# First transform stage: the kernel row of each pair ahead of its signal row, from row 4 on

## The chip, the cores and the metric

The kernel runs on one core of a Trainium2 chip. The time is device microseconds of one execution of the whole program. A core has five engines that work side by side: TensorE (matmuls; PE in the profile, its weight loads PEld), VectorE (DVE), ScalarE (ACT), GpSimd (POOL) and SyncE (SP). Each takes its own instructions in the order in which they were built. SP, ScalarE and GpSimd also issue DMA transfers.

## The reference

Four residual layers, A, B, A, B, on `x` of 2048 rows and 576 columns, each on the layer-normed `x`:

```python
def _A_ref(x, ...):                      # Fourier mixing
    a = einsum("bsd,ed->bse", x, dft_hid_re)
    b = einsum("bsd,ed->bse", x, dft_hid_im)
    return einsum("ts,bse->bte", dft_seq_re, a) - einsum("ts,bse->bte", dft_seq_im, b)

def _B_ref(q, k, v, shift_k, ssm_k, ssm_D):
    k_shift = short causal convolution of k with 4 taps
    kv = k_shift * v
    y = causal convolution of kv with ssm_k over all 2048 rows, by FFT
    return q * (y + kv * ssm_D)          # q is the layer-normed x
```

The long convolution depends on `k`, `v` and `ssm_k` alone and not on `x`. So the kernel computes it once, as a side branch, while the first A layer runs.

## The kernel before

Every float32 operand of a matmul is taken as a high part and a low part. `split` (lines 97 to 99) makes them: ScalarE rounds the source to the high part, and then VectorE subtracts it from the source to get the low part. The products high by high, high by low and low by high are accumulated.

**The main line.** `layer` runs steps n = 0, 1, 2, ...; a step multiplies one 128-row slice of `x` by one 128 by 512 tile of the sequence matrix. `load_c` (L168 is its DMA on SP) fetches the tile into a raw buffer and splits it. It is called two steps ahead and has three split buffers. The text writes C(n) for the tile of step n. A step has 14 matmuls (tiles `s` and `rm` in the profile). Blocks of 16 steps end with the evacuation of the sums into `u`.

**The side branch.** `branch` is a generator. Until step 42 the main loop takes pieces from it after half steps and whole steps, by a fixed schedule (`F1_16`, `F1_END`). Its first stage, the one that is changed, handles 16 rows j of two kinds: the signal row (src 0, `v` times the short convolution of `k`) and the kernel row (src 1, `ssm_k`). The list `todo` gives their order, one entry for two pieces. Rows 0 to 3 (`K_FIRST` = 4) come kind by kind, one row at a time. From row 4 on the two kinds of a row follow each other, and are multiplied together as a pair.

- `f1_loads` (L418 is the load of a row, on SP) keeps three entries ahead. There are three landing buffers (`land`), used in turn, so the load of an entry waits until the third entry before it has been read for the last time. With a row's first entry comes its matrix, by GpSimd (L172).
- `f1_split` makes the parts. For a signal row VectorE first multiplies the landed `v` into the convolved row, in place (L426); this is the last reader of its landing buffer. For a kernel row the last reader is the subtraction of the split. A pair of rows shares one buffer (`xp`, two of them); the first entry of a pair takes it.
- `f1_products` multiplies: a group of six matmuls into two of three PSUM banks (`bf`), two evacuations by ScalarE (L451) and one store to `td` on ScalarE's queue (L452). A pair has three groups of 384 columns, and their turn is set in `visits`, from three half steps behind the pair's second entry on. A row of the first four has two groups of 288 columns.
- `convolve` is the short convolution on VectorE: multiplies at L393, adds at L398. Its operations are spread evenly until the next signal row needs them; `later` in the main loop of the stage finds that row in `todo`. L374 loads `k`.

The order in which each engine gets its instructions is not the order of the source alone: the framework moves an instruction that it expects to be ready ahead of another one. The built order of each engine is fixed before the run.

Of the kernel before, what the change touches and what calls it, by code (L numbers as in the profile page):

```python
# [19 lines left out]
J = S // P  # L20
# [10 lines left out]
K_FIRST = 4  # L31
# [34 lines left out]
def fnet_h3_kernel(ctx: ExitStack, tc: tile.TileContext, x, c_mat, w_re, w_im, k_pad, v, shift_k,  # L66
# [30 lines left out]
    def split(h, l, src):  # L97
        a = nc.scalar.activation(h, src, AF.Copy).ins  # L98
        return a, nc.vector.tensor_tensor(l, src, h.bitcast(F32), OP.subtract).ins  # L99
# [43 lines left out]
    def two(v):  # L143
        return v.rearrange("p (a n) -> p a n", a=2)
# [197 lines left out]
    def parts(i):  # L342
        v = ring[i]()
        return v[:, :D], v[:, D:]
# [4 lines left out]
    def branch():  # L349
# [49 lines left out]
                        yield  # L399

        todo = [(1, 1), (0, 1)] + [(j, 1) for j in range(2, K_FIRST)] + [(j, 0) for j in range(K_FIRST)]
        todo += [(j, src) for j in range(K_FIRST, J) for src in range(2)]
        loads = [0]

        def f1_loads(upto):
            while loads[0] < min(upto, len(todo)):
                j, src = todo[loads[0]]
                loads[0] += 1
                if j not in fcs:
                    fcs[j] = two(ring["fc"]())  # L410
                    if pows:
                        load_fr(fcs[j], f1c[j])
                    else:
                        raw = two(tmp[:, :2 * P])
                        nc.sync.dma_start(raw, f1c[j])
                        nc.scalar.activation(fcs[j], raw, AF.Copy)
                landed[j, src] = ring["land"]()
                nc.sync.dma_start(landed[j, src], (ssm_k if src else v)[:, j, :])  # L418
                if src and j == 0:
                    nc.sync.dma_start(tmp[:1, D:], ssm_d[None, :])  # L420

        def f1_split(j, src):
            r = landed.pop((j, src))
            if not src:
                row = rows[j // 2][:, j % 2, :]
                nc.vector.tensor_tensor(row, row, r, OP.mult)  # L426
                r = row
            elif j == 0:
                nc.vector.tensor_tensor(r[:1], r[:1], tmp[:1, D:], OP.add)
            if j < K_FIRST:  # L430
                xf = parts("xf")
                parted[:] = split(xf[0], xf[1], r)
                return xf
            if not src:
                t = ring["xp"]()
                paired[:] = t[:, :2 * D], t[:, 2 * D:]
            h, l = (t.rearrange("p (a s d) -> p a s d", a=2, s=2)[:, :, src, :] for t in paired)
            parted[:] = split(h, l, two(r))
            return tuple(paired)
# [15 lines left out]
        def visit(half):  # L455
            if visits and visits[0][0] <= half:
                f1_products(*visits.pop(0)[1:])

        for n, (j, src) in enumerate(todo):
            f1_loads(n + 1)  # L460
            if n < 2:
                yield
            xf = f1_split(j, src)
            if j < K_FIRST:
                visits += [(2 * n + 2, j, fcs[j], xf, hf * HD, HD, "so", hf * D + src * HD) for hf in range(2)]
            elif src:
                visits += [(2 * n + 3, j, fcs[j], xf, at, VW, "sp", at) for at in range(0, 2 * D, VW)]
            if n:
                f1_loads(n + 3)
            later = [m for m in range(n + 1, len(todo)) if todo[m][1] == 0 and 7 * (todo[m][0] // 2 + 1) > made_ops]  # L470
            for half in range(2):
                visit(2 * n + half)
                if later and n > 2:
                    left = 7 * (todo[later[0]][0] // 2 + 1) - made_ops
                    for _ in range(-(-left // (2 * (later[0] - n) - half)) if left > 0 else 0):
                        next(conv)
                        made_ops += 1
                yield
# [267 lines left out]
    pending = []  # L746
    lay(flts, SC_AT, ("craw", NT, CRAW))
    br = branch()
    wl = load_w()
    load_x(0)  # L750
# [404 lines left out]
```

## Time and profile before

| | |
|---|---|
| median of 3 runs | 1191.76 us (1188.8 to 1192.48) |
| the profiled execution | 1191.32 us |
| its span | 1189.5 us |
| granted TensorE clock, mean | 0.998 |
| TensorE matmuls busy | 1168.5 us |
| VectorE busy | 872.8 us |
| ScalarE busy | 650.0 us |
| the stage that is changed, from the first pair's first group to its last group | 94.2 to 198.6 us |

A row of the order of time begins with the start in us, then the duration in us, the engine, the line, the operation, the tiles (written <- read), shapes and a count of equal instructions in a row. In brackets stands the idle time of the engine just before, and what ended it. A "q" behind an engine's name marks its queue, which issues a DMA. In the view by windows each engine has its busy us and instructions in the stretch, in the order PE, PEld, DVE, ACT, POOL; the last three figures are the granted clock, the share of the DMA engines and GB/s. In the DMA views the last figure is the median us from issue to landing.

### The profile page before, as it was taken

What the parts mean: (1) busy time and instruction counts of PE and PEld (TensorE: products, weight loads), DVE (VectorE), ACT (ScalarE), POOL (GpSimd) and SP (SyncE); (2) the same over time, 40 slices, a digit from 0 to 9 for tenths busy, and PEclk for the clock granted to TensorE, in tenths of its full rate; (3) what the DMA queues carried; (4) which work ended last, traced back from release to release, by engine and by line L of the source; (5) the groups of instructions that cost most, each with busy time, mean ns of one, the idle gap of its engine ahead of it and who ended that gap; (6) DMA issues with size and microseconds to landing.
All of it is one profiled execution on the core that took longest, in us unless ns stands there. A gap on an engine that the chain in (4) does not pass through costs nothing.

```text
span 1189.5 us, 18071 instructions
## 1 busy us (share of the span) xinstructions
PE 1168.5 (98%) x6184; PEld 987.2 (83%) x6184; DVE 872.8 (73%) x1562; ACT 650.0 (55%) x1279; POOL 75.1 (6%) x116
## 2 busy tenths in 40 slices
PE   7999999999999999999999999999999999999997
PEld 5776767888888888888888898888888888889997
DVE  7899983688777778787767665865776776775764
ACT  7865555567766668766645666534444445450200
POOL 2210000000000000001101111000000000001111
PEclk9999999999999999999999999999999999999999
DMA  9869898545656656648966777772772776795621
GB/s 340 295 197 306 269 290 267 178 139 177 225 189 198 200 160 204 186 137 239 273 197 226 235 246 231 251 250 73 255 248 71 240 273 248 266 322 158 214 83 41
DMA packets 147454, 255.65 MB, mean 215 GB/s; under 512 B 16161, under 2 KB 56353, under 8 KB 147362
## 3 DMA queue, kind: packets, MB, share of 16 engines
q1 hardware_dynamic: 111890, 210.17, 54.9%
q10 hardware_dynamic: 28560, 37.91, 9.1%
q0 software_dynamic: 6912, 6.43, 2.4%
q8 instruction: 48, 0.79, 0.3%
q14 instruction: 44, 0.36, 0.1%
HBM read 187.80 MB, written 66.65 MB: 214 GB/s over the span
## 4 chain that ended last, share of the span: by engine, by line
PE 76%; ACT 2%; DVE 2%; DMA 2%; issue 1%; POOLq 0%; ACTq 0%; DVEq 0%
PE s L75 42%; PE bk L75 29%; PE rm L75 4%; ACT flts L512 1%; ACT mid L512 1%; DMA t<-ud 1%; DVE mid L518 0%; DMA yb<-flts 0%; DMA flts<-vd 0%; DMA flts<-in_c_mat 0%; DVE flts L532 0%; DVE flts L530 0%; ACT u L98 0%; DVE flts L531 0%; DVE flts L533 0%
## 5 line engine op out<-in xcount | busy, mean ns | idle before, releaser
L75 PE MATMUL s<-mats 128*128 128x512 f32 x2088 | 543.0, 395 | 1.6 <-ACT mats L195 0.8
L75 PEld LDWEIGHTS s<-mats 128*128 128x128 f32 x2088 | 381.0, 188 | 83.2 <-issue 10.6
L99 DVE TENSOR_TENSOR mats<-flts,mats 128x512 fp32r<-128x512 f32 x206 | 141.0, 688 | 50.8 <-ACT mats L98 48.4
L98 ACT ACTIVATE mats<-flts 128x512 fp32r<-128x512 f32 x206 | 128.3, 628 | 82.6 <-PE bk L75 31.2
L75 PE MATMUL bk<-mid 128*128 128x288 f32 x704 | 127.7, 302 | 1.6 <-DVE flts L287 0.8
L75 PEld LDWEIGHTS bk<-mid 128*128 128x128 f32 x704 | 108.0, 188 | 23.7 <-ACT flts L512 5.8
L512 ACT ACTIVATE flts<-bk 128x288 f32<-128x288 f32 (+1 forms) x192 | 76.3, 406 | 90.8 <-PE bk L75 75.9
L75 PE MATMUL bk<-w,u 128*128 128x288 f32 x864 | 121.3, 296 | 1.0 <-DVE w L241 0.4
L75 PEld LDWEIGHTS bk<-w,u 128*128 128x128 f32 x864 | 117.3, 188 | 5.5 <-DVE flts L532 1.7
L518 DVE TENSOR_TENSOR mid<-flts,mid 128x576 fp32r<-128x576 f32 (+1 forms) x149 | 93.4, 629 | 18.6 <-ACT mid L512 15.2
L75 PE MATMUL rm<-mats 128*128 128x512 f32 x304 | 94.6, 391 | 0.2 <-ACT flts L512 0.2
L512 ACT ACTIVATE mid<-flts 128x576 fp32r<-128x576 f32 (+1 forms) x148 | 80.3, 575 | 11.8 <-DVE flts L533 8.5
L287 DVE TENSOR_TENSOR flts<-flts,bk 128x288 f32<-128x288 f32 x48 | 21.8, 453 | 65.8 <-PE bk L75 65.7
L451 ACT ACTIVATE flts<-bf 128x384 f32<-128x384 f32 (+1 forms) x104 | 43.2, 463 | 46.0 <-PE bf L75 45.9
L75 PE MATMUL bk<-mats 128*128 128x288 f32 (+1 forms) x376 | 67.8, 317 | 0.0
L75 PEld LDWEIGHTS rm<-mats 128*128 128x128 f32 x304 | 56.9, 188 | 12.8 <-ACT flts L512 0.6
L75 PE MATMUL s<-t,mats 128*128 128x512 f32 x264 | 65.4, 390 | 0.6 <-DVE t L99 0.3
L184 POOL TENSOR_TENSOR flts<-flts 128x1 f32<-128x1 f32 x35 | 28.7, 821 | 522.4 <-DVE flts L183 522.3
L75 PE MATMUL bk<-mats,t 128*128 128x288 f32 (+1 forms) x368 | 59.3, 303 | 0.0
L512 ACT ACTIVATE flts<-flts 64x288 f32<-64x288 f32 x128 | 56.6, 443 | 4.7
L75 PEld LDWEIGHTS s<-t,mats 128*128 128x128 f32 x264 | 49.4, 188 | 11.7 <-DVE t L99 0.8
L75 PEld LDWEIGHTS bk<-mats 128*128 128x128 f32 x376 | 55.5, 188 | 3.4
(146 smaller groups left out, 1496.7 us busy)
## 6 DMA issues: line engine op xcount, KB each, us to landing
flts<-in_c_mat SPq DMA_DIRECT2D x148, 256.0 KB, 3.3
ph<-in_c_mat SPq DMA_DIRECT2D x54, 512.0 KB, 4.5
flts<-in_c_mat SPq DMA_DIRECT2D x30, 512.0 KB, 4.8
flts<-td SPq DMA_DIRECT2D x53, 288.0 KB, 2.9
td<-flts ACTq DMA_DIRECT2D x36, 384.0 KB, 4.6
vd<-flts ACTq DMA_DIRECT2D x64, 144.0 KB, 2.7
flts<-vd SPq DMA_DIRECT2D x32, 288.0 KB, 4.1
ud<-ph ACTq DMA_DIRECT2D x12, 512.0 KB, 6.3
```

The source lines that it names most:

```text
L75: return nc.tensor.matmul(ps, lhsT, rhs, start=first, stop=last, skip_group_check=more).ins
L98: a = nc.scalar.activation(h, src, AF.Copy).ins
L99: return a, nc.vector.tensor_tensor(l, src, h.bitcast(F32), OP.subtract).ins
L184: pows.append(nc.gpsimd.tensor_tensor(rs, ve, mhalf, OP.pow).ins)
L287: added[:] = [nc.vector.tensor_tensor(r[:, cs], r[:, cs], ps[:, :HD], OP.add).ins]
L451: stored[:] = [nc.scalar.activation(so[:, i, :], ps[i], AF.Copy).ins]
L512: last_act.append(nc.scalar.activation(*args, **kw).ins)
L518: nc.vector.tensor_tensor(l, src, h.bitcast(F32), OP.subtract)
```

## The change

From row 4 on, the entry of the kernel row stands ahead of that of the signal row. The kernel row takes the pair's buffer, and the three groups are due behind the signal row.

```diff
         todo = [(1, 1), (0, 1)] + [(j, 1) for j in range(2, K_FIRST)] + [(j, 0) for j in range(K_FIRST)]
-        todo += [(j, src) for j in range(K_FIRST, J) for src in range(2)]
+        todo += [(j, src) for j in range(K_FIRST, J) for src in (1, 0)]
...
-            if not src:
+            if src:
                 t = ring["xp"]()
                 paired[:] = t[:, :2 * D], t[:, 2 * D:]
...
             if j < K_FIRST:
                 visits += [...]
-            elif src:
+            elif not src:
                 visits += [(2 * n + 3, j, fcs[j], xf, at, VW, "sp", at) for at in range(0, 2 * D, VW)]
```

## The prediction

> **What bounds the kernel now.** I read the page first, then the busy time by windows, then the order of time around rows 3 to 6 of the first transform stage, and last the DMA views. Names: a "step" n is the 14 matmuls on one sequence-matrix tile C(n); a "group" is the six matmuls of one call of `f1_products`, numbered 0 to 51 in issue order, so groups 14 and 15 are the two halves of signal row 3, groups 16 to 18 row 4, 19 to 21 row 5. kernel(j) and signal(j) are the two splits of row j; product(j) is the multiply at L426 before signal(j).
>
> ```profile
> span 1189.5 us, 18071 instructions
> PE 1168.5 (98%) x6184; PEld 987.2 (83%) x6184; DVE 872.8 (73%) x1562; ACT 650.0 (55%) x1279; POOL 75.1 (6%) x116
> PE 76%; ACT 2%; DVE 2%; DMA 2%; issue 1%; POOLq 0%; ACTq 0%; DVEq 0%
> ```
>
> ```profile
> 80.00:100.00 20.00, 18.54 (x96) 13.20 (x94) 19.44 (x24) 9.31 (x21) 1.05 (x2) 1.00 0.85 257
> 100.00:120.00 20.00, 20.00 (x102) 14.08 (x99) 20.00 (x23) 11.47 (x24) 1.58 (x3) 1.00 0.98 332
> 180.00:200.00 20.00, 20.00 (x102) 14.08 (x103) 6.86 (x10) 11.78 (x24) 0.53 (x1) 1.00 0.75 242
> ```
>
> TensorE bounds the run; in the stage of the change VectorE (third figure) is nearly as full, and after 180 us it is two thirds idle. How full TensorE really is comes from the starts of the groups:
>
> ```profile
> 79.07 0.68 PE L75 MATMUL bf<-f1r 64*128 64x288 f32 x6
> 80.88 0.66 PE L75 MATMUL bf<-f1r 64*128 64x288 f32 x6 [0.24 <-ACT flts L451]
> 85.79 0.67 PE L75 MATMUL bf<-f1r 64*128 64x288 f32 x6
> 87.29 0.66 PE L75 MATMUL bf<-f1r 64*128 64x288 f32 x6
> 94.24 0.79 PE L75 MATMUL bf<-f1r 64*128 64x384 f32 x6
> 97.38 0.79 PE L75 MATMUL bf<-f1r 64*128 64x384 f32 x6 [1.22 <-ACT flts L451]
> 107.94 0.79 PE L75 MATMUL bf<-f1r 64*128 64x384 f32 x6
> 112.08 0.79 PE L75 MATMUL bf<-f1r 64*128 64x384 f32 x6
> 114.39 0.79 PE L75 MATMUL bf<-f1r 64*128 64x384 f32 x6
> 197.84 0.80 PE L75 MATMUL bf<-f1r 64*128 64x384 f32 x6
> ```
>
> These are groups 12 to 17, 21 to 23 and 51. By the built order 14 step matmuls stand between groups 21 and 22 and six between 22 and 23: 4.14 = 14m + g and 2.31 = 6m + g, so m = 0.229 us for a step matmul and g = 0.94 us for a group. From group 17 to 51 there are 300 step matmuls and 34 groups: 68.7 + 32.0 = 100.7 us, and the rows give 197.84 - 97.38 = 100.46. So TensorE waits for nothing after group 17. Between 16 and 17 stand four step matmuls: 0.94 + 0.92 = 1.86 against 3.14, a stall of 1.28 us. Between 12 and 13 some 0.38 us is lost. No more than 1.7 us can be won here. What causes both:
>
> ```profile
> 75.73 0.33 SPq L418 DMA_DIRECT2D flts<-in_ssm_k  x1
> 79.54 0.69 ACT L98 ACTIVATE f1r<-flts 128x576 fp32r<-128x576 f32 x1 [2.00 <-DMA flts<-in_ssm_k]
> 80.13 0.69 ACT L451 ACTIVATE flts<-bf 128x288 f32<-128x288 f32 x2
> 86.49 0.71 ACT L451 ACTIVATE flts<-bf 128x288 f32<-128x288 f32 x2 [2.45 <-PE bf L75]
> 90.43 0.33 SPq L418 DMA_DIRECT2D flts<-in_ssm_k  x1
> 95.89 0.68 ACT L98 ACTIVATE f1r<-flts 128x576 fp32r<-128x576 f32 x1 [4.76 <-DMA flts<-in_ssm_k]
> 96.47 0.85 ACT L451 ACTIVATE flts<-bf 128x384 f32<-128x384 f32 x2
> ```
>
> ScalarE takes its queue in order. kernel(4) and kernel(5) stand there ahead of the evacuations of groups 12 and 16; it waits for their loads (landing 79.54 - 75.73 = 3.81 us and 95.89 - 90.43 = 5.46 us after issue), the evacuations come late, and the next group finds no free bank of the three.
>
> **The change, part by part.** Nothing is added or removed: each pair keeps two loads, one product, two ScalarE and two VectorE splits, three groups. From step 48 on every engine's built order is the same, and up to group 13 TensorE's is. GpSimd's is unchanged. What moves:
>
> (1) The three landing buffers. A load takes the buffer of the third load before it in the list. kernel(j) used to wait for product(j-1) and now waits for product(j-2); signal(j) used to wait for the split of kernel(j-2) and now waits for that of kernel(j-1). kernel(4) takes the old slot of the signal and is there long before its turn: the 0.38 us at group 13 goes.
>
> (2) ScalarE's order, which decides the sum:
>
> ```
> before: C20, store, signal(3), evacuate 14, store, evacuate 15, C21, C22, store, signal(4), kernel(5), evacuate 16
> after:  C20, signal(3), store, kernel(5), evacuate 14, store, evacuate 15, C21, store, C22, signal(4), evacuate 16
> ```
>
> kernel(5) no longer stands before group 16, so the 1.28 us goes; but now it stands before group 14's evacuation, which group 15 waits for. Its load waits on SP for the matrix load ahead of it and for product(3):
>
> ```profile
> 79.57 2.16 SPq L168 DMA_DIRECT2D flts<-in_c_mat  x2
> 79.43 1.35 DVE L398 TENSOR_TENSOR f1f<-f1f 128x1152 f32<-128x1152 f32 x1
> 80.70 0.68 DVE L99 TENSOR_TENSOR mats<-flts,mats 128x512 fp32r<-128x512 f32 x1
> 81.31 1.34 DVE L393 TENSOR_TENSOR f1f<-f1f 128x1152 f32<-128x1152 f32 x1
> 82.57 0.75 DVE L426 TENSOR_TENSOR f1f<-f1f,flts 128x576 f32<-128x576 f32 x1
> 83.24 1.34 DVE L398 TENSOR_TENSOR f1f<-f1f 128x1152 f32<-128x1152 f32 x1
> 83.34 0.33 SPq L418 DMA_DIRECT2D flts<-in_v  x1
> ```
>
> The L426 row is product(3); SP issues the signal load 0.02 us after it ends. In the changed order product(3) stands before the L393 multiply, so it runs at 81.31 and ends at 82.06; the matrix loads are issued by 81.73; kernel(5) is issued at 82.08. How long it then takes is the one unknown. Bounds:
>
> ```profile
> flts<-in_v SPq DMA_DIRECT2D x1, 288.0 KB, 5.2
> ...
> f1f<-in_k_pad SPq DMA_DIRECT2D x2, 576.0 KB, 6.2
> ```
>
> The first row is the 288 KB load issued at 83.34, through the same crowd of transfers; the second the 576 KB loads of 70 to 100 us. 3.81 us (the load at 75.73, mostly clear of the crowd) is the low end, 6.2 the high end. I take 5.3, between the nearest rows 5.2 and 5.46: landing at 87.4. ScalarE then copies it (95.89 to 96.47, 0.58 to the next start), evacuates group 14 (0.71 for both) and is done at 88.7; TensorE follows 0.06 us later (80.13 + 0.69 to 80.88): group 15 starts at 88.75. Without that wait: group 13 at 80.50, then 4.91 us as from 80.88 to 85.79 less four step matmuls, as group 14 now stands after 268 of them and not 272: 84.5, or 84.65 since its VectorE split ends at 80.70 + 0.61 + 0.67 + 1.26 + 0.61 + 0.75 = 84.6; then 1.50 as from 85.79 to 87.29: 86.15. So the new stall is 2.6 us. At the same place in the matmul order group 15 of before is at 87.29 - 4 x 0.229 = 86.37; the change is 2.4 us late there.
>
> [...]
>
> (3) Group 17 then finds free banks: group 16 comes 31 step matmuls and one 288-wide group (1.50 - 0.69 = 0.81) after 88.75, at 96.66, evacuated 0.1 + 0.85 us after its 0.79 at 98.4; group 17 is due at 98.5. The 1.28 us is saved: 2.4 - 1.28 = 1.1 us late.
>
> (4) VectorE does the same work in another order, convolution up to one step later; after 180 us it has the room. What covers the delay is the lead of a step's low half over its use:
>
> ```profile
> 129.45 0.69 DVE L99 TENSOR_TENSOR mats<-flts,mats 128x512 fp32r<-128x512 f32 x1
> 136.32 1.67 PE L75 MATMUL s<-mats 128*128 128x512 f32 x6
> ```
>
> C(30) is split at 130.14 for a use at 136.32: 6.2 us. If that cover were gone each microsecond late would count.
>
> (5) signal(j)'s load is later, which is the slower rival below. Priced at nothing here: it stays under the cover of (4).
>
> Nothing behind 200 us has an order of its own to lose, so 1.1 us carries to the end. The profiled execution took 1191.32 us, 0.44 below the median 1191.76 of the runs; with 1.1 it gives 1192.4, and the median 1192.9. With the bounds of the landing: -0.4 us (3.81) to +2.0 us (6.2), so 1191.4 to 1193.8.
>
> **The rivals.** *No new wait*: the load lands by 84.9, ahead of its turn. Against it, no row nearby is that fast; for it, the crowd is partly of this kernel's own stores, whose order shifts. Gain 0.2 + 1.28 = 1.5 us: 1190.3.
>
> *The wait slows the clock*: TensorE idles 2.6 us at one place.
>
> ```profile
> 96.00:98.00 2.00, 0.78 (x7) 0.47 (x6) 2.00 (x3) 1.85 (x4) 0.00 (x0) 1.00 0.82 260
> ```
>
> After 1.22 us idle the granted clock is still 1.00, which speaks against it. Were it halved for as long as the gap, 2.6 us of matmuls would take 1.3 more: 1194.2. [...]
>
> *Slower: VectorE waits for signal loads.* In the changed order the buffer of signals 7, 9 and 10 is freed by the split of kernels 6, 8 and 9, and four operations (a convolution multiply, an add, a matrix split and a row split or product) stand before each product: 1.26 + 1.27 + 0.61 + 0.67 = 3.8 us. Before, signal(7) had ten:
>
> ```profile
> 102.64 0.33 SPq L418 DMA_DIRECT2D flts<-in_v  x1
> 112.68 0.76 DVE L426 TENSOR_TENSOR f1f<-f1f,flts 128x576 f32<-128x576 f32 x1
> ...
> DMA to landing us min/median/max: 2.8/4.1/7.3
> ```
>
> At the median landing 0.3 us is lost three times, under the 6.2 us of lead; at the maximum 3.5 us three times, 10.5 in all, and 4.3 us reach TensorE: 1192.9 + 4.3 = 1197.2. It decides once the three landings average over 5.9 us.
>
> *It does nothing that shows*: a wait of about the old size at the new place, within the range of the forecast.
>
> **How the numbers follow.** A difference of 0.3% (3.6 us) is about what a measurement of this kernel can tell from no change; the shown runs spread by that. Forecast, "nothing that shows" included, with its own range 1191.4 to 1193.8: 0.61. No new wait: 0.15, of which 0.04 ends below 1188.2. Clock: 0.06, of which 0.02 ends above 1195.3. VectorE waits: 0.18, of which 0.15 ends there. Slower is 0.02 + 0.15 + 0.01 for the forecast's own tail = 0.18, faster 0.04, same 0.78. The range runs from the no-wait case less a third of the spread of the runs (1188.8 to 1192.48) to most of the VectorE case: 1189 to 1196.3.
>
> **What would show it.** Right: ScalarE idle some 4 us before the kernel(5) copy near 87.4 us, released by its load; group 15 at about 88.7 after a wait of 2 to 3 us; no wait at group 17; group 51 near 199; VectorE waiting for signal loads under 1 us at a time; the clock at 1.00. Wrong: group 15 by 86.3 (no wait), waits of TensorE for step splits between 110 and 165 us (the VectorE rival), or a changed distance from group 51 to the end.

## The result and the profile after

The changed kernel takes 1195.14 us (median of 6 runs, 1194.92 to 1197.25); the kernel before takes 1190.6 us (6 runs, 1188.8 to 1192.48). The ratio is 1.0042, 95% interval 1.0031 to 1.0053: 4.5 us slower. The profiled execution took 1194.96 us, 3.6 us more than the profiled one of before. The page of the changed kernel, its span, engines and chain:

```profile
span 1193.0 us, 18074 instructions
PE 1170.0 (98%) x6184; PEld 988.1 (83%) x6184; DVE 872.5 (73%) x1562; ACT 649.6 (54%) x1279; POOL 75.1 (6%) x116
PE 73%; ACT 3%; DVE 2%; DMA 2%; issue 1%; ACTq 0%; POOLq 0%; DVEq 0%
```

The totals tell nothing of the cause. The order of time in the changed kernel does: groups 13 to 17 and 51, product(3) (L426), and the load and the copy of kernel(5):

```profile
80.53 0.66 PE L75 MATMUL bf<-f1r 64*128 64x288 f32 x6
81.27 0.74 DVE L426 TENSOR_TENSOR f1f<-f1f,flts 128x576 f32<-128x576 f32 x1
82.04 0.33 SPq L418 DMA_DIRECT2D flts<-in_ssm_k  x1
84.61 0.66 PE L75 MATMUL bf<-f1r 64*128 64x288 f32 x6
88.31 0.68 ACT L98 ACTIVATE f1r<-flts 128x576 fp32r<-128x576 f32 x1 [5.28 <-DMA flts<-in_ssm_k]
88.90 0.69 ACT L451 ACTIVATE flts<-bf 128x288 f32<-128x288 f32 x2
89.64 0.77 PE L75 MATMUL bf<-f1r 64*128 64x288 f32 x6 [3.48 <-ACT flts L451]
99.03 0.80 PE L75 MATMUL bf<-f1r 64*128 64x384 f32 x6
100.88 0.79 PE L75 MATMUL bf<-f1r 64*128 64x384 f32 x6
201.37 0.80 PE L75 MATMUL bf<-f1r 64*128 64x384 f32 x6
```

ScalarE stands 5.28 us before the copy of kernel(5), with the evacuation of group 14 behind it, and TensorE waits 3.48 us at group 15. Two distances from this list tell the rest. From group 16 to 17 it is 1.85 us, so the old wait of 1.28 us is gone. From group 15 to 16 it is 9.39 us for 31 step matmuls; in the kernel before it was 6.95 us for 27, which four more at 0.23 us make 7.87. So 1.5 us were lost in which TensorE was never idle. The view by windows of the changed kernel shows where (first TensorE's busy time, third figure from the end the granted clock):

```profile
83.24:86.65 3.41, 2.93 (x15) 1.69 (x14) 3.41 (x6) 0.00 (x0) 0.00 (x0) 1.00 1.08 346
86.65:90.06 3.41, 0.42 (x6) 0.42 (x6) 3.41 (x4) 1.28 (x3) 0.00 (x0) 1.00 0.55 195
90.06:93.47 3.41, 3.41 (x11) 2.50 (x10) 2.08 (x4) 1.23 (x3) 0.53 (x1) 0.50 0.71 219
93.47:96.89 3.42, 3.42 (x16) 2.82 (x15) 2.65 (x5) 1.21 (x2) 0.00 (x0) 1.00 0.87 274
```

Behind the gap the granted clock is 0.50 for 3.41 us, and full again after it. Seven step matmuls took 3.31 us there (from 90.35 us), 0.47 each against 0.23 at full clock. Half the matmuls of 3.41 us are 1.7 us.

The account, against the kernel before: -0.35 us at group 13, +3.5 us at group 15, +1.5 us of half clock, -1.3 us at group 17, in sum 3.4 us; the last 0.1 us is lost between groups 13 and 14. Group 51 is 201.37 - 197.84 = 3.53 us late, the span 3.5 us longer. All of the difference of the two profiled executions arose between 79 and 101 us, from group 12 to group 17.

### The profile page after: what moved, and what is told of

Read it like the earlier page. It is cut to its first block, busy times and chain, and to the rows that moved or that the text cites. A ratio compares the mean times of both kernels' runs of the same rounds, so it can differ in the third digit from the quotient of the medians.

```text
span 1193.0 us, 18074 instructions
## 1 busy us (share of the span) xinstructions
PE 1170.0 (98%) x6184; PEld 988.1 (83%) x6184; DVE 872.5 (73%) x1562; ACT 649.6 (54%) x1279; POOL 75.1 (6%) x116
## 4 chain that ended last, share of the span: by engine, by line
PE 73%; ACT 3%; DVE 2%; DMA 2%; issue 1%; ACTq 0%; POOLq 0%; DVEq 0%
PE s L75 41%; PE bk L75 28%; PE rm L75 4%; ACT flts L512 1%; ACT mid L512 1%; DVE mid L518 1%; DMA flts<-vd 1%; DMA t<-ud 1%; DMA yb<-flts 0%; ACT mats L98 0%; DVE flts L532 0%; DVE flts L531 0%; DVE flts L530 0%; DMA flts<-in_c_mat 0%; DMA flts<-td 0%
```

## The experiments

**Which rows.** The theory is one wait, at the place where the pairs begin; the rival is that every pair costs, through late signal loads on VectorE. The first two runs split the change by rows.

```diff
-        todo += [(j, src) for j in range(K_FIRST, J) for src in (1, 0)]
+        todo += [(j, src) for j in range(K_FIRST, J) for src in ((1, 0) if j < 6 else (0, 1))]
...
```

The two conditions of the change (the pair's buffer and its groups) follow the order of their row.

> Kernel row ahead of signal row for rows 4 and 5 alone, the old order from row 6 on. Theory (one wait): all of the loss is here, TensorE waits about 3.5 us at group 15 with the half clock behind it, ratio 1.003 to 1.005. Rival (every pair): two pairs of twelve, ratio about 1.0007.

Measured 1.0040, interval 1.0027 to 1.0054: the whole loss with two pairs of twelve. In its order of time, the copy of kernel(5) and group 15:

```profile
87.86 0.68 ACT L98 ACTIVATE f1r<-flts 128x576 fp32r<-128x576 f32 x1 [4.86 <-DMA flts<-in_ssm_k]
89.19 0.66 PE L75 MATMUL bf<-f1r 64*128 64x288 f32 x6 [3.07 <-ACT flts L451]
```

The other half has `j >= 6` in the same place.

> Kernel row ahead of signal row from row 6 on, the old order for rows 4 and 5. Theory (one wait): none of the loss is here, the 1.28 us wait at group 17 is still there, ratio 0.999 to 1.001. Rival (every pair): ten pairs of twelve, ratio about 1.0035.

Measured 1.0003, interval 0.9994 to 1.0011: no loss with ten pairs of twelve. The old wait is still there, at group 17 behind kernel(5):

```profile
95.26 0.68 ACT L98 ACTIVATE f1r<-flts 128x576 fp32r<-128x576 f32 x1 [4.79 <-DMA flts<-in_ssm_k]
96.75 0.44 PE L75 MATMUL bf<-f1r 64*128 64x384 f32 x2 [1.34 <-ACT flts L451]
```

The rival of every pair falls.

**Which cause.** The next two keep the changed order of all rows and take the wait away, once by the load and once by the queue. The first multiplies product(3) right behind product(2):

```diff
-                nc.vector.tensor_tensor(row, row, r, OP.mult)
+                for i in {2: (2, 3), 3: ()}.get(j, (j,)):
+                    o = rows[i // 2][:, i % 2, :]
+                    nc.vector.tensor_tensor(o, o, landed.get((i, 0), r), OP.mult)
```

> The changed kernel, with the product of row 3 multiplied right behind that of row 2 (some 5 us earlier on VectorE), so that the buffer for the load of kernel row 5 comes free and the load is issued near 76 us instead of 82.04 us. Theory (one wait): the 3.5 us wait of TensorE at group 15 and the 1.5 us of half clock behind it go, and the old 1.28 us at group 17 and 0.37 us at group 13 stay gone, so the time is 1.6 us below the kernel before: ratio 0.998 to 0.9995. Rival (the order of every pair costs, through late signal loads on VectorE): nothing that counts changes, ratio about 1.004 as for the changed kernel.

Measured 1.0002, interval 0.9994 to 1.0011. The load of kernel(5) is issued at 76.97, its copy waits for nothing, and group 15, which the built order puts five step matmuls earlier here, does not wait:

```profile
76.97 0.33 SPq L418 DMA_DIRECT2D flts<-in_ssm_k  x1
82.80 0.69 ACT L98 ACTIVATE f1r<-flts 128x576 fp32r<-128x576 f32 x1
85.57 0.66 PE L75 MATMUL bf<-f1r 64*128 64x288 f32 x6
94.56 0.79 PE L75 MATMUL bf<-f1r 64*128 64x384 f32 x6
96.40 0.80 PE L75 MATMUL bf<-f1r 64*128 64x384 f32 x6
```

The loss is gone. The expected gain of 1.6 us over the kernel before is not there, though: this kernel waits 0.80 us elsewhere, at 122.7 us, and the interval ends short of the full 1.6 us.

The second leaves the load where it is and holds the splits of kernel(5) behind the evacuation of group 15 (`stored`, the last one built):

```diff
-            parted[:] = split(h, l, two(r))
+            with behind(*(stored if (j, src) == (5, 1) else ())):
+                parted[:] = split(h, l, two(r))
```

> The changed kernel, with the two splits of kernel row 5 held behind the evacuation of group 15 in the engines' order; its load is where the changed kernel has it and still lands near 88 us. Theory (one wait): it is the place in ScalarE's queue that costs and not the late landing, so groups 15 and 17 start without a wait, the clock stays at 1.00 and the time is 1.6 us below the kernel before: ratio 0.998 to 0.9995. Rival (every pair): ratio about 1.004.

Measured 0.9994, interval 0.9985 to 1.0003, median 1190.19 us. Groups 15 to 17 with the copy between:

```profile
87.00 0.66 PE L75 MATMUL bf<-f1r 64*128 64x288 f32 x6
89.25 0.69 ACT L98 ACTIVATE f1r<-flts 128x576 fp32r<-128x576 f32 x1 [0.31 <-DMA flts<-in_ssm_k]
95.30 0.79 PE L75 MATMUL bf<-f1r 64*128 64x384 f32 x6
97.14 0.79 PE L75 MATMUL bf<-f1r 64*128 64x384 f32 x6
```

The load lands as late as in the changed kernel, near 89 us, and nobody minds: 1.84 us from group 16 to 17, no wait, the clock at full. So it is the place in ScalarE's queue that costs, and not the landing alone. This kernel is clearly faster than the changed one; that it is faster than the kernel before, as its 1.3 us less of waits would have it, the interval neither shows nor excludes. None of the runs is clearly faster than the kernel before.

The traces are finer here than the times. From the start of group 11 to that of group 51 TensorE has the same number of matmuls in all four kernels. The stretch takes 122.53 us in the kernel before (75.31 to 197.84), 126.09 in the changed one (75.28 to 201.37), 121.84 with the early product (75.91 to 197.75) and 121.48 with the copy behind (76.20 to 197.68). So in one trace each the two repaired kernels did gain 0.7 and 1.05 us in this stage.

**How long a gap it takes, and what sets the landing.** Five runs keep the changed kernel's built order. Up to here the granted clock had fallen behind a gap of 3.48 us (group 15 of the changed kernel) and not behind one of 1.22 us (group 17 of the kernel before). Two shorten the load of kernel(5) itself:

```diff
-                nc.sync.dma_start(landed[j, src], (ssm_k if src else v)[:, j, :])
+                c = D // 2 if (j, src) == (5, 1) else D
+                nc.sync.dma_start(landed[j, src][:, :c], (ssm_k if src else v)[:, j, :c])
```

> The changed kernel with the same built order, but the load of kernel row 5 moves only the first 288 of its 576 columns (144 KB); the other half of the row is left as the buffer had it, so this row of the transform is not the reference's. Theory (the clock falls only after a gap of about 3.4 us): the load lands some 0.7 us earlier, the gap at group 15 is 2.6 to 3.0 us, and the granted clock stays at 1.00; the time is 2.2 us below the changed kernel, ratio about 1.002. Rival (any gap of over 2 us lowers the clock): the half clock stays for about as long as the gap, ratio 1.003 or more.

> As the run with 288 columns, but only 72 of the 576 columns of kernel row 5 are loaded (36 KB); the rest of the row is left as the buffer had it. Theory: the load lands near 87.0 us behind the matrix load ahead of it in its queue, the gap is 2.0 to 2.4 us and the clock stays at 1.00, ratio about 1.001. Rival: the half clock stays, ratio 1.002 or more.

Measured 1.0055 (1.0036 to 1.0074) with half of it and 1.0027 (1.0010 to 1.0044) with an eighth. The trace of the eighth:

```profile
81.22 0.33 SPq L418 DMA_DIRECT2D flts<-in_ssm_k  x1
87.43 0.68 ACT L98 ACTIVATE f1r<-flts 128x576 fp32r<-128x576 f32 x1 [5.23 <-DMA flts<-in_ssm_k]
88.76 1.09 PE L75 MATMUL bf<-f1r 64*128 64x288 f32 x6 [3.43 <-ACT flts L451]
```

The expectation was wrong twice. 36 KB took 6.2 us from issue to the copy, as 288 KB did in the changed kernel (88.31 - 82.04 = 6.3); 144 KB took 5.8 us (82.22 to 88.06), with a gap of 3.06 us. And the granted clock fell to 0.50 behind both gaps, where full clock was expected. Of the other three runs two shorten the load of 576 KB that is issued on the same queue 4 us ahead, and one repeats the changed kernel as it is. From 82.04 to 88.31 us, while the load of kernel(5) was under way, the changed kernel's transfers moved 332 GB/s in all.

```diff
-                nc.sync.dma_start(ks[:, at:at + 2 * D], k_pad[:, 2 * i * D:2 * (i + 1) * D])
+                c = D if i == 6 else 2 * D               # D // 4 in the second kernel
+                nc.sync.dma_start(ks[:, at:at + c], k_pad[:, 2 * i * D:2 * i * D + c])
```

> The changed kernel with the same built order; the one load of convolution input that is issued some 4 us ahead of that of kernel row 5, on the same queue, moves 288 KB instead of 576 (the other half of that buffer stays as it was, so two rows of the short convolution are not the reference's). Theory (the landing is set by what is queued ahead, not by the transfer's own size): kernel row 5 lands 288 KB / 320 GB/s = 0.9 us earlier, the gap of TensorE at group 15 is about 2.6 us. The clock then falls where the gap fills most of one of its 3.41 us periods, which hangs on the run: ratio 1.0015 to 1.003. Rival (a fixed latency of its own): the gap stays at 3.1 to 3.5 us, ratio about 1.004.

> As before, but that load moves 72 KB of its 576 (the rest of its buffer stays as it was, so two rows of the short convolution are not the reference's). Theory: kernel row 5 lands 1.6 us earlier, the gap is about 1.9 us and mostly too short for the clock to fall: ratio 1.000 to 1.001. Rival (a fixed latency of its own): the gap stays at 3.1 to 3.5 us, ratio about 1.004.

> The changed kernel once more, on the chip of the two runs above. Theory: the gap at group 15 is 3.1 to 3.6 us and covers at least half of a 3.41 us period wherever it falls, so the clock falls each time: ratio 1.003 to 1.005, and one half-clock stretch of 3.41 us near 90 us in the trace. Rival (the fall of the clock was one run's chance): full clock in this trace, ratio about 1.002.

Measured 1.0036 (1.0023 to 1.0049), 1.0028 (1.0018 to 1.0037) and 1.0044 (1.0028 to 1.0060). The gaps at group 15 were 3.44, 2.70 and 2.64 us: half the load ahead changed nothing, and an eighth gave a gap no shorter than that of the repeated kernel. In these two runs the load ahead is also issued earlier, at 76.50 and 76.00 us instead of 78.23. The rows are of the eighth and then of the repeated kernel:

```profile
81.08 0.33 SPq L418 DMA_DIRECT2D flts<-in_ssm_k  x1
86.57 0.68 ACT L98 ACTIVATE f1r<-flts 128x576 fp32r<-128x576 f32 x1 [4.50 <-DMA flts<-in_ssm_k]
87.90 0.67 PE L75 MATMUL bf<-f1r 64*128 64x288 f32 x6 [2.70 <-ACT flts L451]
```

```profile
82.19 0.33 SPq L418 DMA_DIRECT2D flts<-in_ssm_k  x1
87.62 0.68 ACT L98 ACTIVATE f1r<-flts 128x576 fp32r<-128x576 f32 x1 [4.41 <-DMA flts<-in_ssm_k]
88.96 0.66 PE L75 MATMUL bf<-f1r 64*128 64x288 f32 x6 [2.64 <-ACT flts L451]
```

So the unchanged kernel's own landing moves between 5.4 and 6.3 us (in two executions, which may have been on different chips), and neither the bytes of the load nor those ahead of it on its queue brought it out of that span. The packet times of the traces narrow it a little. With an eighth of the load, 112 of its 128 packets had started 3.6 us after issue (by 84.86 us), with half of it 4.4 us (by 86.61); but the last eight started only 5.1 to 5.8 us after issue with an eighth (86.30 to 86.98), and 4.7 to 5.3 us with half. Most of the smaller load came earlier, and its last packets did not. What holds these back stays open.

The clock is not open. It fell to 0.50 behind group 15 in all seven traces that have the wait, and stayed at 1.00 there in the four that have not. Its changes lie on a grid of 3.41 us (in the repeated kernel the falls at 89.92 and 219.62 us are 38 periods apart), and where the grid lies against the work differs from run to run (the first falls are at 87.84 to 90.44 us). The periods just before a fall, of the repeated kernel (two, and behind the second the period at half clock), of the run with rows 4 and 5 alone and of the run with half the load ahead; then the idlest periods near 215 us of the kernel before and of the run with the early product, behind which it did not fall; and last two periods near the end of a run, with an eighth of kernel(5)'s load and with half the load ahead, behind which it did not fall either:

```profile
86.51:89.92 3.41, 0.96 (x8) 0.76 (x9) 3.41 (x5) 1.55 (x4) 0.00 (x0) 1.00 0.61 213
216.21:219.62 3.41, 1.16 (x7) 0.93 (x7) 1.97 (x3) 1.31 (x2) 0.00 (x0) 1.00 0.51 154
219.62:223.03 3.41, 3.41 (x14) 3.02 (x13) 1.79 (x3) 0.24 (x1) 0.00 (x0) 0.50 0.53 151
```

```profile
216.53:219.95 3.42, 1.31 (x8) 1.10 (x9) 1.65 (x3) 1.31 (x2) 0.00 (x0) 1.00 0.50 143
```

```profile
215.18:218.59 3.41, 1.43 (x9) 0.99 (x8) 1.24 (x3) 1.95 (x4) 0.00 (x0) 1.00 0.56 127
```

```profile
213.06:216.47 3.41, 2.37 (x13) 1.49 (x11) 2.05 (x4) 0.92 (x2) 0.00 (x0) 1.00 0.48 149
```

```profile
213.69:217.10 3.41, 2.05 (x10) 1.41 (x10) 2.13 (x5) 1.28 (x2) 0.00 (x0) 1.00 0.49 141
```

```profile
1183.52:1186.93 3.41, 1.56 (x12) 1.32 (x10) 1.71 (x5) 0.00 (x0) 0.29 (x1) 1.00 0.00 0
```

```profile
1184.56:1187.98 3.42, 1.67 (x13) 1.43 (x11) 1.61 (x5) 0.00 (x0) 0.19 (x1) 1.00 0.00 0
```

In the eleven traces, from the first record of the clock near 15 us on, TensorE was busy for 1.43 us or less of the 3.41 us before each fall, that is idle for 58% or more, and for 1.56 us or more, idle for 54% or less, in every period at full clock behind which it held.

A second fall, near 219 us, came in three of the seven traces with the wait and in none of the other four. There TensorE waits 1.7 to 1.9 us for the last hidden-matrix tile, whose load took 7.7 us in the repeated kernel. Wait and fall together cost some 2 us: from group 51 to the end is 1193.0 - 201.4 = 991.6 us in the changed kernel's first trace and 1194.5 - 200.7 = 993.8 us in the repeated one. Two of the changed kernel's six runs took 1197.2 us at a mean clock of 0.996, the other four 1194.9 to 1195.2 us at 0.997; a second fall may be what sets the two apart, but they have no trace. Whether the first wait favours the second one, or it was chance in so few traces, was not tried. That the medians differ by 4.5 us and the traces by 3.5 comes for 0.7 us from the kernel before, whose profiled execution lay above its median (1191.32 against 1190.6 us).

## Why the prediction was right or wrong

The time lies in the range, at its upper end, but on the slower side of 0.3%, which had a chance of 0.18; the forecast was 1.1 us late and 4.5 us were measured. That the range held it was in part luck: its upper end of 1196.3 us was set by the rival of VectorE's waits, which did not happen, and the forecast's own range ended at 1193.8, below the measured 1195.14. Point by point:

- *TensorE bounds the stage and waits nowhere behind group 17*: right. All but 0.1 us of what the changed kernel loses and wins lies at groups 13, 15 and 17, the half clock behind group 15 with it.
- *Part 1 and part 3, the old waits go*: right, 0.35 and 1.3 us.
- *Part 2, kernel(5) in front of the evacuation of group 14*: right in place and mechanism, and shown from both sides, by moving the load and by moving the copy. The terms: issue at 82.08, measured 82.04; landing 5.3 us later, measured 6.3 in the first trace and 5.4 in the second; wait 2.6 us, measured 3.5 and 2.64. The end of the bounds taken from the 576 KB loads (6.2) was the better one for the first trace. This term was up to 0.9 us too small.
- *The clock*: wrong, and the largest error. "After 1.22 us idle the granted clock is still 1.00, which speaks against it" set a gap of 2.6 us beside one of 1.22, and the rival got 0.06. Even the forecast gap could be long enough: in the repeated kernel a gap of 2.64 us left 72% of one period idle and brought the half clock. It need not: a gap of 2.6 us that falls half into one period and half into the next would leave an estimated 38% of each idle, and periods idle for up to 54% held. The seven falls behind group 15 followed periods idle for 69 to 93%. The rival's price of 1.3 us, half clock for as long as the gap, was near: the clock stood at 0.50 for 3.41 us in the first trace, and 1.5 us were lost. The forecast of 1.1 us late with the clock's 1.5 would have been 2.6 us late, and with the 0.9 us of the wait 3.5, as the first trace has it.
- *Late signal loads on VectorE*: did not happen. The view of the loads of `v` in the changed kernel, who waited for them and how long they took:

```profile
  DVE f1f L426: 2.3, 1
DMA to landing us min/median/max: 2.9/3.4/6.1
```

One wait of 2.3 us in all, at 183.8 us, where VectorE has room. The sign "under 1 us at a time" did not hold, but the wait lies under the cover of the lead that was named, and the run from row 6 on shows no loss.
- *1.1 us carries to the end*: as a rule right, since nothing behind group 51 gave time back in the first trace; but in three traces a second half-clock stretch near 219 us came on top, which the prediction did not have.

## What to carry to other kernels

Moving a load earlier in the source can move the instruction that waits for it earlier in an engine's queue by more than the load gained; look at what stands behind that instruction, here an evacuation that TensorE needed, and hold the waiting instruction behind it. Price a TensorE wait not only with its own length: in these traces gaps of 1.7 to 3.5 us that left 58% or more of a 3.41 us period idle had a granted clock of 0.50 behind them for one or two such periods, and the one of 3.48 us cost 1.5 us more by it. Where the transfers are crowded (DMA share 1.00 from 82.04 to 88.31 us in the changed kernel), take the slow end of the rows for a landing on which TensorE hangs: here the rows had 3.81 to 6.2 us, and 6.3 and 5.4 were measured.

## What was not expected of the hardware

- The granted clock fell behind periods of 3.41 us in which TensorE was idle for 58% or more (gaps of 1.7 to 3.5 us, the shorter ones with another beside them), and not behind 54% or less. Near groups 15 to 17 and near 219 us it then stayed at 0.50 for one period, or for two with an eighth of kernel(5)'s load (87.84 to 94.67 us); there the wait went on into the first of the two and left 27% of it idle.
- The landing of the load of kernel(5), 6.3 us after issue with 288 KB in the changed kernel, came 6.2 us after issue with 36 KB, and it moved by 0.9 us, to 5.4, in a second execution of the same kernel.
